# Value projections in four column tiles, and two figures of an instruction planner

## The chip, the core and the metric

The kernel runs on one core of a Trainium2 chip. The time is that of the device, in microseconds (us), from runs of the whole kernel. The core has a matrix engine (PE), a scalar engine for exponentials and gelu (ACT), a vector engine (DVE), GpSimd (POOL) and a queue that issues the DMAs (SP). They run on their own and wait for each other by semaphores.

## The reference, cut to what matters

Two layers, each an attention (A) and a token mixer with an MLP (B), on one sequence of 2048 tokens of 512 features. All 32 heads have 16 features and share one key and one value projection.

```
x = x + A(layernorm(x)); x = x + B(layernorm(x))     # twice, the same weights
A: q = (x @ wq) in 32 heads of 16;  k = x @ wk;  v = x @ wv        # k, v: 2048 x 16
   p = softmax(q k^T / 4);  o = p v;  return o @ wo
B: h = gelu(layernorm(x) @ w1), its four column groups shifted by 1, -1, 2, -2 tokens; x1 = x + h @ w2
   return x1 + gelu(layernorm(x1) @ w3) @ w4
```

## The kernel before

**Attention.** Queries are taken in chunks of 512 tokens (two of 256 at the end of layer 2). A chunk has eight blocks of four heads; a block goes over 16 key tiles of 128. The scores of two heads and one key tile, 128 keys by 1024, are a "half" (two key tiles of 256 queries in the short chunks); there are 2048 halves. Scores are made by row-tiled matmuls (`qk`, L1051), 32 rows each. An exponential is taken in one of two ways. A "unit" (`declare_unit`, L1084) is one ACT instruction over a half (L1100) into one of six EA buffers. A "pair" (`declare_pair`, L1106) takes two DVE instructions that turn scores into the bits of a bf16 power of two (L1121, J, four buffers), and two further versions with added constants (L1131, JK, five buffers), most of them on POOL; the three are weighted by scaled copies of the values (VD). PV (`declare_pv`, L1166) multiplies either by the values, with the values' rows also holding a one, so that the softmax's denominators come out with the sums. Four column tiles of 32 columns accumulate in one PSUM bank per block.

**At a block's end** (`block_end`, L1188) DVE copies the bank (L1214). PE picks the denominators out of the copy (`fz`, L1219 to 1227: four tokens' column tiles for each 128 queries), DVE takes reciprocals (L1231), PE spreads them (L1239), DVE multiplies (L1245), and DMAs move the result to where the output projection reads it.

**Values.** `kv` (L897) makes keys and values of a few token tiles from their normalised, transposed input. Keys are column-tiled (L909). Values (`fv`, L924 to 932) are tokens by features: the tokens are the weights of the array, 128 columns, and WV streams through with 32 columns; four such matmuls sum over the 512 features. DVE copies the 16 used columns (L933) and makes three scaled copies (L938). There are 11 calls: four of four tiles in layer 1's head, seven of one to four tiles between the layers.

**The order of instructions** is written out by a planner in the program itself (`Plan`, L32). Each operation has a duration, a priority and what it reads and writes. The planner simulates the engines, picks at each moment the operation of best priority that it holds ready, and emits for each engine a fixed order with semaphore waits. On the chip the order stands, and only the times differ. What bears on the change:

- A PE operation has a kind: "Q" for row-tiled scores, "P" for column-tiled work, "F" for the whole array. Its planned time is a count of columns at 2.4 per ns; kind P adds 6 ns for each 512 columns. A change of kind costs 0.103 us in the plan (`SWITCH`), and an operation can join those in flight only if its kind is theirs (L224).
- PVs wait until two are ready before a run of kind P is begun for them (`deferred`, L266), or until one has waited for 3 us.
- Where PE would otherwise not be busy enough, the planner puts in matmuls of zeros, fillers (L1062).
- An operation's result counts as ready at its end less `after`, plus a drain (0 for POOL); a reader on PE may start 0.06 us after that (L377, L162 to 172). The engine itself is taken for the whole duration. A POOL instruction at L1131 is planned with 1.12 us.
- Pairs are started when PSUM banks, buffers and DVE's planned queue allow (`assign`, L1312). How many halves become pairs thus comes out of the plan.

Of the kernel before, what the change touches and what calls it, by code (L numbers as in the profile page):

```python
# [31 lines left out]
class Plan:  # L32
# [70 lines left out]
    def op(self, eng, emit, reads=(), writes=(), dur=0.1, prio=None, take=None, give=None,  # L103
           dma=0, out=False, side=True, pe=None, port=False, parts=1, after=0.0):
        o = Op()
        o.eng, o.emit, o.dur, o.take, o.give, o.dma, o.out, o.side = \
            eng, emit, dur, take, give, dma, out, side
        o.pe = pe
        o.port = port
        o.parts = parts  # L110
        o.after = after
        o.feeds = None
        o.seq = len(self.ops)
        o.prio = self.base if prio is None else prio
        o.succ = []
        o.placed = False
        o.start = o.end = None
        o.pos = None
        preds = set()
        for t in reads:  # L120
            r = self.res.get(t)
            if r is not None and r[0] is not None:
                preds.add(r[0])
        for t in writes:
            r = self.res.get(t)
            if r is not None:
                if r[0] is not None:
                    preds.add(r[0])
                preds.update(r[1])
        for t in reads:  # L130
            self.res.setdefault(t, [None, []])[1].append(o)
        for t in writes:
            self.res[t] = [o, []]
        o.preds = preds
        for t in writes:
            if isinstance(t, Late):
                if take is None:
                    t.gates += [p for p in preds if p not in t.ops]
                t.ops.append(o)
        o.ready = self.now  # L140
        o.entry = 0.0
        if self.pace is not None and side:
            if pe is not None:
                self.release += pe[1] * self.pace / 2400.0
                if take is not None:
                    self.entry = self.release
            o.entry = self.entry
        n = 0
        for p in preds:
            if p.placed:  # L150
                o.ready = max(o.ready, self._after(p, o))
            else:
                p.succ.append(o)
                n += 1
        o.npend = n
        self.ops.append(o)
        self.left += 1
        if n == 0:
            self._push(o)
        return o  # L160
# [349 lines left out]
def t_x4(n):  # L510
    return 0.068 + n * 0.26e-3
# [18 lines left out]
class Kernel:  # L530
# [366 lines left out]
    def kv(self, la, tiles, prio=None):  # L897
        op = self.pl.op
        slot = self.slot(la, tiles[0] // 4)
        n0 = (tiles[0] % 4) * 128  # L900
        n = 128 * len(tiles)
        rd = self.yt_tags(la, tiles)
        L = Late()
        for h in range(2):
            def fpe(e, h=h):
                ins = None
                for dc in (2 * h, 2 * h + 1):
                    for g in range(4):
                        ins = e.matmul(self.PB[32 * g:32 * g + 32, L.bank, 0:n], lhsT=self.WK[:, dc, :],  # L909
                                       rhs=self.yt(slot)[:, dc, n0:n0 + n], start=(dc == 0), stop=(dc == 3),  # L910
                                       tile_position=(0, 32 * g), skip_group_check=True)
                return ins
            op("PE", fpe, reads=rd + [("WK",)], writes=[L], pe=("P",) + mm(n, 2)[1:] + (range(4),), prio=prio,
               take=L if h == 0 else None)
        k0 = tiles[0] * 128
        if la == 0 and tiles[0] == 0:
            op("ACT", lambda e: e.copy(self.KT[:, la, k0:k0 + n], self.PB[:, L.bank, 0:n]),
               writes=[L] + [("KT", la, t) for t in tiles], dur=0.0505 + n / 1200, prio=prio, give=L)
        else:
            op("DVE", lambda e: e.tensor_copy(self.KT[:, la, k0:k0 + n], self.PB[:, L.bank, 0:n]),  # L920
               writes=[L] + [("KT", la, t) for t in tiles], dur=t_ps(n), prio=prio, give=L)
        M = Late()

        def fv(e):  # L924
            ins = None
            for i, tb in enumerate(tiles):
                for dc in range(4):
                    ins = e.matmul(self.PB[:, M.bank, 32 * i:32 * i + 32],
                                   lhsT=self.yt(slot)[:, dc, n0 + i * 128:n0 + (i + 1) * 128],
                                   rhs=self.WV[:, dc, :], start=(dc == 0), stop=(dc == 3))  # L930
            return ins
        op("PE", fv, reads=rd + [("WV",)], writes=[M], pe=("F", 240 * len(tiles), 128 * len(tiles)), prio=prio, take=M)
        op("DVE", lambda e: e.tensor_copy(  # L933
            self.VP[:, la, tiles[0]:tiles[0] + len(tiles), 0:16],
            self.PB[:, M.bank, 0:32 * len(tiles)].rearrange("p (t x) -> p t x", x=32)[:, :, 0:16]),
           writes=[M] + [("VP", la, t) for t in tiles], dur=0.14, prio=prio)
        for j in range(3):
            op("DVE", lambda e, j=j: e.tensor_scalar(  # L938
                out=self.VD[:, j, la, tiles[0]:tiles[0] + len(tiles), 0:16],
                in0=self.PB[:, M.bank, 0:32 * len(tiles)].rearrange("p (t x) -> p t x", x=32)[:, :, 0:16],  # L940
                scalar1=self.PARTS[j], scalar2=None, op0=ALU.mult),
               writes=[M] + [("VD", la, t) for t in tiles], dur=0.14, prio=prio, give=M if j == 2 else None)
# [163 lines left out]
    def declare_pair(self, g):  # L1106

        op = self.pl.op  # L1110
        m = self.ndve
        self.ndve += 1
        self.waiting.append(m)
        js = m % self.N_J
        J = self.J[:, js, :]
        for i in range(2):
            h = 2 * g[5] + i
            L = Late()
            op("PE", lambda e, h=h, L=L: self.qk(e, g, h, L.bank), reads=self.inputs(g), writes=[L],
               pe=("Q", 512, 128, (h,)), prio=0.5, side=False, take=L)  # L1120
            o = op("DVE", lambda e, i=i, L=L: e.tensor_scalar(  # L1121
                out=J[:, i * 512:(i + 1) * 512], in0=self.PB[:, L.bank, :],
                scalar1=128 * LOG2E * 0.25, scalar2=float(127 * 128), op0=ALU.mult, op1=ALU.add),
                writes=[L, ("J", js, i)], dur=t_ps(512), prio=1, side=False, give=L)
        jt = [("J", js, 0), ("J", js, 1)]
        es = [(J, jt)]
        for k in (1, 2):
            r = (2 * m + k - 1) % self.N_JK
            self.adds = [p for p in self.adds if not p.placed]
            eng = "POOL" if len(self.adds) < self.ADDS else "DVE"  # L1130
            x = op(eng, lambda e, k=k, r=r: e.tensor_scalar(  # L1131
                out=self.JK[:, r, :], in0=J, scalar1=float(self.STEPS[k]), scalar2=1.0, op0=ALU.add,
                op1=ALU.mult),
               reads=jt, writes=[("JK", r)], dur=t_x4(1024) if eng == "DVE" else 1.12, prio=2, side=False, port=True,
                   after=0.0 if eng == "DVE" else 0.07)
            if eng == "DVE":
                o = x
            else:
                self.adds.append(x)
            es.append((self.JK[:, r, :], [("JK", r)]))  # L1140
        self.pairs.append(o)
        self.add_pv(g, [(self.shaped(ap.bitcast(dt.bfloat16), [2, 512]), tg, k, m) for k, (ap, tg) in enumerate(es)])
# [45 lines left out]
    def block_end(self, la, c, b, end):  # L1188
        op = self.pl.op
        if end == "more":  # L1190
            ap, tags = self.SPILL[b]
            self.last_copy = op("DVE", lambda e: e.tensor_tensor(out=ap, in0=self.PB[:, self.ACC, :], in1=ap,
                                                                 op=ALU.add),
                                writes=[("AC",)] + tags, dur=t_ps(512), prio=0, side=False)
            return
        if end == "spill":
            ap, tags = self.SPILL[b]
            self.last_copy = op("DVE", lambda e: e.tensor_copy(ap, self.PB[:, self.ACC, :]), writes=[("AC",)] + tags,
               dur=t_ps(512), prio=0, side=False)
            return  # L1200
        n = self.size(la, c)
        nq = n // 128
# [3 lines left out]
        am, zm, om = ([(x, i) for i in parts] for x in ("ACCF", "RZ", "OS"))  # L1206
        acc, rz, osm = self.ACCF[:, m * n:m * n + n], self.RZ[:, 4 * nq * m:4 * nq * (m + 1)], self.OS[:, m * n:m * n + n]
        if end == "add":
# [3 lines left out]
               reads=tags, writes=[("AC",)] + am, dur=t_ps(512), prio=0, side=False)  # L1212
        else:
            self.last_copy = op("DVE", lambda e: e.tensor_copy(acc, self.PB[:, self.ACC, 0:n]),  # L1214
               writes=[("AC",)] + am, dur=t_ps(n), prio=0, side=False)
        fin = min(5, self.RUSH[la][c])
        L = Late()

        def fz(e):  # L1219
# [4 lines left out]
                    ins = e.matmul(self.PB[32 * g:32 * g + 32, L.bank, 4 * q:4 * q + 4], lhsT=acc[:, y:y + 32],  # L1224
                                   rhs=self.SELC, start=True, stop=True, tile_position=(0, 32 * g))
            return ins
        op("PE", fz, reads=am + [("SELC",)], writes=[L], pe=("P", 100 * nq, 4 * nq, range(4)), prio=fin, take=L)

        def frec(e):
            with self.nc.allow_low_precision("the reciprocals feed a bf16 matmul"):  # L1230
# [349 lines left out]
```

## Time and profile before

| | |
|---|---|
| time, median of 9 runs | 1534.26 us (1533.68 to 1534.59) |
| the profiled execution: its own time, its span | 1534.59 us, 1532.8 us |
| busy: PE, ACT, DVE, POOL | 98%, 96%, 84%, 76% |
| exponentials on ACT (L1100) | 1471 |
| DVE conversions (L1121), two for a pair | 1154 |
| JK on POOL, on DVE (L1131) | 982, 172 |
| value matmuls (L928), whole array | 128 |
| denominator matmuls (L1224), in 72 sums | 1024 |
| fillers on PE (ones by zeros) | 952 matmuls, 86.9 us busy |

Busy times are of one profiled execution. A matmul's record includes its way through the array, so records overlap, and PE's share is not a share of its peak; what one matmul takes from the next is read from the distance of their starts. A line such as `x1471 | 1353.7, 1152 | 16.1` gives the number of instructions, their busy time in us, the mean of one in ns, and the engine's idle time before them in us, followed by what ended it. The chain that ended last goes back from the last instruction to what released it, step by step. PEld is the weight load of PE, which overlaps with its matmuls.

### The profile page before, as it was taken

The page shows a single profiled execution, that of the slowest core. Times are in us where ns is not written, and L with a number is a line of the kernel's source. Part 1 is how long each engine was busy: PE and PEld are TensorE (multiplying, and loading weights), DVE is VectorE, ACT ScalarE, POOL GpSimd, SP SyncE. Part 2 cuts the span into 40 slices and gives each one's busy share as a digit, 9 for nine tenths or more (in the row PEclk, how much of TensorE's full clock was granted, in tenths as well). Part 3 has the DMA queues.
Part 4 walks back from the last instruction along what each step waited for, and adds up shares of the span by engine and source line. Part 5 has one row for each costly group of instructions (what it writes and reads, how often), then busy time and mean ns, then how long its engine had stood idle before and what let it go on. Part 6 is the DMA issues. An engine that isn't in the chain of part 4 may idle for free.

```text
span 1532.8 us, 66274 instructions
## 1 busy us (share of the span) xinstructions
PE 1495.2 (98%) x30137; PEld 648.8 (42%) x30137; DVE 1282.1 (84%) x2265; ACT 1469.8 (96%) x1563; POOL 1171.7 (76%) x1243
## 2 busy tenths in 40 slices
PE   8999999999999999999999999999999999999999
PEld 4333333443433444333434434334443334454565
DVE  8888888889988889988886788988788896898863
ACT  7999999999999989999999999999999999999972
POOL 2789999878888858987675489888788886788651
DMA  6100100001000001000000000010000000000000
GB/s 208 30 5 5 20 6 6 4 6 19 6 4 6 6 4 20 6 5 2 3 2 3 3 8 11 6 20 4 13 14 7 5 6 11 19 10 7 6 14 23
DMA packets 32153, 21.70 MB, mean 14 GB/s; under 512 B 12672, under 2 KB 31360, under 8 KB 31872
## 3 DMA queue, kind: packets, MB, share of 16 engines
q1 hardware_dynamic: 31872, 17.47, 4.8%
q8 instruction: 235, 3.85, 1.1%
q14 instruction: 46, 0.38, 0.1%
HBM read 7.90 MB, written 2.10 MB: 7 GB/s over the span
## 4 chain that ended last, share of the span: by engine, by line
ACT 75%; PE 15%; POOL 6%; DVE 3%; issue 1%; DMA 0%; SPq 0%; POOLq 0%
ACT EA L1100 70%; PE PB L653 6%; POOL JK L1131 4%; PE PB L1056 4%; PE PB L1180 3%; ACT G L1513 2%; ACT L1100 1%; DVE J L1121 1%; ACT GP L1433 1%; POOL SM L788 1%; ACT L1433 1%; POOL ZR L1404 1%; ACT L1513 1%; DMA X<-in_A_x_dram 0%; DVE G L1508 0%
## 5 line engine op out<-in xcount | busy, mean ns | idle before, releaser
L1100 ACT ACTIVATE EA<-PB 128x1024 bf16<-128x1024 f32 x1471 | 1353.7, 1152 | 16.1 <-PE PB L1180 10.3
L1131 POOL TENSOR_SCALAR JK<-J 128x1024 uint16<-128x1024 uint16 x982 | 1036.6, 1056 | 253.1 <-DVE J L1121 160.5
L1121 DVE TENSOR_SCALAR J<-PB 128x512 uint16<-128x512 f32 x1154 | 745.2, 681 | 120.3 <-PE PB L1056 117.5
L1056 PE MATMUL PB<-QT,KT 32*128 32x512 bf16 (+1 forms) x4608 | 614.3, 360 | 19.8 <-ACT EA L1100 8.3
L1180 PE MATMUL PB<-EA,VP 128*32 128x256 bf16 (+1 forms) x6636 | 381.9, 263 | 1.9 <-DVE ACCF L1214 1.2
L1056 PEld LDWEIGHTS PB<-QT,KT 32*128 32x128 bf16 x4608 | 163.4, 91 | 400.8 <-ACT EA L1100 335.1
L1180 PE MATMUL PB<-JK,VD 128*32 128x256 bf16 (+1 forms) x5160 | 301.3, 266 | 5.2 <-POOL JK L1131 3.6
L1180 PEld LDWEIGHTS PB<-EA,VP 128*32 128x32 bf16 x6636 | 157.5, 95 | 136.4 <-issue 105.7
L1180 PEld LDWEIGHTS PB<-JK,VD 128*32 128x32 bf16 x5160 | 119.2, 94 | 145.2 <-issue 81.6
L653 PE MATMUL PB<-ZT,W 128*32 128x512 bf16 (+2 forms) x2816 | 173.2, 342 | 0.8 <-DVE ZT L861 0.3
L1180 PE MATMUL PB<-J,VD 128*32 128x256 bf16 (+1 forms) x2580 | 164.8, 264 | 0.6 <-issue 0.3
L1131 DVE TENSOR_SCALAR JK<-J 128x1024 uint16<-128x1024 uint16 x172 | 121.2, 712 | 3.0 <-PE PB L1180 0.4
L653 PE MATMUL PB<-W,G 128*32 128x512 bf16 x1624 | 102.4, 380 | 0.1
L653 PE MATMUL PB<-ONES,NIL 128*32 128x512 bf16 x952 | 86.9, 391 | 3.2 <-DVE ST L768 0.9
L1508 DVE CAST G<-PB 128x512 bf16<-128x512 f32 (+2 forms) x126 | 71.8, 580 | 20.2 <-PE PB L653 19.4
L1180 PEld LDWEIGHTS PB<-J,VD 128*32 128x32 bf16 x2580 | 64.2, 95 | 43.2 <-issue 34.5
L653 PEld LDWEIGHTS PB<-ZT,W 128*32 128x32 bf16 x2816 | 61.6, 96 | 37.3 <-issue 23.5
L788 POOL TENSOR_TENSOR SM<-SM,MH 128x2 f32<-128x2 f32 (+1 forms) x69 | 48.0, 698 | 22.8 <-DVE SM L790 16.0
L1513 ACT ACTIVATE G<-G 128x1792 bf16<-128x1792 bf16 x29 | 47.0, 1686 | 12.6 <-DVE G L1508 12.5
L653 PEld LDWEIGHTS PB<-W,G 128*32 128x32 bf16 x1624 | 42.3, 96 | 36.3 <-issue 10.9
L1245 DVE TENSOR_TENSOR OS<-ACCF,PB 128x512 bf16<-128x512 bf16 (+1 forms) x72 | 44.6, 619 | 7.1 <-PE PB L1239 6.9
L768 DVE BATCH_NORM_STATS2 ST<-X 128x6 f32<-128x512 f32 (+1 forms) x64 | 43.3, 681 | 3.1 <-DMA X<-in_A_x_dram 2.5
(108 smaller groups left out, 865.0 us busy)
## 6 DMA issues: line engine op xcount, KB each, us to landing
OT<-OS SPq DMA_DIRECT2D x424, 8.0 KB, 1.8
W<-in_B_w_dram SPq DMA_DIRECT2D x2, 1792.0 KB, 14.1
X<-in_A_x_dram SPq DMA_DIRECT2D x8, 256.0 KB, 6.7
QT<-QS SPq DMA_DIRECT2D x32, 64.0 KB, 2.5
out_dram<-OUTB SPq DMA_DIRECT2D x16, 128.0 KB, 1.7
OT<-OS SPq DMA_DIRECT2D x104, 4.0 KB, 2.2
W<-in_B_w_dram SPq DMA_DIRECT2D x2, 512.0 KB, 8.6
WQ<-in_A_wq_dram SPq DMA_DIRECT2D x1, 512.0 KB, 6.2
```

The source lines that it names most:

```text
L653: ins = e.matmul(self.PB[32 * g:32 * g + 32, bank, 0:n], lhsT=lhsT[:, 32 * g:32 * g + 32], rhs=rhs, start=start, stop=stop, tile_position= ...
L768: op("DVE", lambda e, tb=tb: e.bn_stats(self.ST6[:, tb, :], src(tb)), reads=[tagf(tb)], writes=[("ST", tb)], dur=0.606, prio=prio)
L788: op("POOL", lambda e: e.tensor_tensor(out=out, in0=src, in1=self.MH[:, 0, a:b], op=ALU.pow), reads=tags + [("MH",)], writes=tg(r), dur=0. ...
L1056: ins = e.matmul(self.PB[:, bank, j * n:(j + 1) * n], lhsT=self.KT[32 * h:32 * h + 32, la, (kb + j) * 128:(kb + j + 1) * 128], rhs=self.QT ...
L1100: o = q.feeds = op("ACT", lambda e: e.activation(self.EA[:, ea, :, :], self.PB[:, b0:b0 + 2, :], ACTF.Exp, scale=0.25), writes=bk + [("EA" ...
L1121: o = op("DVE", lambda e, i=i, L=L: e.tensor_scalar(out=J[:, i * 512:(i + 1) * 512], in0=self.PB[:, L.bank, :], scalar1=128 * LOG2E * 0.25 ...
L1131: x = op(eng, lambda e, k=k, r=r: e.tensor_scalar(out=self.JK[:, r, :], in0=J, scalar1=float(self.STEPS[k]), scalar2=1.0, op0=ALU.add, op1 ...
L1180: ins = e.matmul(self.PB[32 * x:32 * x + 32, self.ACC, p * hw:p * hw + hw], lhsT=v[:, la, kb + j, :], rhs=ap[:, i, j * w + u * hw:j * w + ...
L1245: op("DVE", lambda e: e.tensor_tensor(out=osm, in0=acc, in1=self.PB[:, M.bank, 0:n], op=ALU.mult), reads=am, writes=[M] + om, dur=t_ps(n), ...
L1433: op("ACT", lambda e: e.activation(self.GP[:, par, :, 2:2 + n], self.GP[:, par, :, 2:2 + n], ACTF.Gelu_apprx_tanh), reads=gt, writes=gt, d ...
L1508: op("DVE", lambda e, f=f, L=L: e.tensor_copy(self.G2[:, f, 0:n], self.PB[:, L.bank, 0:n]), writes=[L] + [(x, f, i) for x in ("G2", "GE") ...
L1513: op("ACT", lambda e, i=i: e.activation(self.G2[:, :, i * 128:(i + 1) * 128], self.G2[:, :, i * 128:(i + 1) * 128], ACTF.Gelu_apprx_tanh), ...
```

## The change

Three edits. Values: each whole-array matmul becomes four column-tiled ones, with 32 tokens as the weights of each column tile; they write the same places of the bank, and the planner has them as kind P with 256 columns for each token tile, where it had kind F with 240. Denominator sums: their planned columns go from 100 to 60 for each 128 queries; the instructions are the same. JK on POOL: `after` is dropped, so a result counts as ready at 1.12 us from its start, where it was 1.05. The last two change what the planner believes, and all three the order that it writes.

```
                 for dc in range(4):
-                    ins = e.matmul(self.PB[:, M.bank, 32 * i:32 * i + 32],
-                                   lhsT=self.yt(slot)[:, dc, n0 + i * 128:n0 + (i + 1) * 128],
-                                   rhs=self.WV[:, dc, :], start=(dc == 0), stop=(dc == 3))
+                    for g in range(4):
+                        y = n0 + i * 128 + 32 * g
+                        ins = e.matmul(self.PB[32 * g:32 * g + 32, M.bank, 32 * i:32 * i + 32],
+                                       lhsT=self.yt(slot)[:, dc, y:y + 32], rhs=self.WV[:, dc, :], start=(dc == 0),
+                                       stop=(dc == 3), tile_position=(0, 32 * g), skip_group_check=True)
             return ins
-        op("PE", fv, reads=rd + [("WV",)], writes=[M], pe=("F", 240 * len(tiles), 128 * len(tiles)), prio=prio, take=M)
+        op("PE", fv, reads=rd + [("WV",)], writes=[M], pe=("P", 256 * len(tiles), 128 * len(tiles), range(4)), prio=prio, take=M)
...
-               reads=jt, writes=[("JK", r)], dur=t_x4(1024) if eng == "DVE" else 1.12, prio=2, side=False, port=True,
-                   after=0.0 if eng == "DVE" else 0.07)
+               reads=jt, writes=[("JK", r)], dur=t_x4(1024) if eng == "DVE" else 1.12, prio=2, side=False, port=True)
...
-        op("PE", fz, reads=am + [("SELC",)], writes=[L], pe=("P", 100 * nq, 4 * nq, range(4)), prio=fin, take=L)
+        op("PE", fz, reads=am + [("SELC",)], writes=[L], pe=("P", 60 * nq, 4 * nq, range(4)), prio=fin, take=L)
```

## The prediction

> **What bounds the kernel now.** I read the page's busy shares first, then the chain that ended last, then the groups of instructions, then the waits, and last the timeline around the lines that the diff touches.
>
> ```profile
> span 1532.8 us, 66274 instructions
> PE 1495.2 (98%) x30137; PEld 648.8 (42%) x30137; DVE 1282.1 (84%) x2265; ACT 1469.8 (96%) x1563; POOL 1171.7 (76%) x1243
> ACT 75%; PE 15%; POOL 6%; DVE 3%; issue 1%; DMA 0%; SPq 0%; POOLq 0%
> ```
>
> The first two lines are the page's totals, the third its chain by engine. PE shows 98%, but it holds 952 matmuls of ones times zeros, fillers that the planner puts in where PE has nothing due: 238 groups of four, about 0.215 us apart, some 51 us. So ScalarE is the bound: three quarters of the chain is on it. The other 25% are stretches in which the chain runs through PE, POOL and DVE and ScalarE is served just in time; only there is a nanosecond of PE or POOL worth a nanosecond.
>
> ```profile
> L1100 ACT ACTIVATE EA<-PB 128x1024 bf16<-128x1024 f32 x1471 | 1353.7, 1152 | 16.1 <-PE PB L1180 10.3
> L1131 POOL TENSOR_SCALAR JK<-J 128x1024 uint16<-128x1024 uint16 x982 | 1036.6, 1056 | 253.1 <-DVE J L1121 160.5
> L1121 DVE TENSOR_SCALAR J<-PB 128x512 uint16<-128x512 f32 x1154 | 745.2, 681 | 120.3 <-PE PB L1056 117.5
> 36.15 172.43 ACT EA L1100 x188
> ```
>
> Three groups of the page and one piece of the chain. There are 2048 halves of score tiles; 1471 go through ScalarE's exponential, and 1154/2 = 577 as "pairs" through DVE and POOL. The chain's piece gives the exponential's pitch, 172.43/188 = 0.917 us. A pair more or less is therefore 0.917 us of ScalarE.
>
> ```profile
> POOL JK L1131 <- PE PB L1180: 20.4, 19, 2.7
> PEld PB L1180 <- POOL JK L1131: 45.2, 166, 0.8
> ACT EA L1100 <- PE PB L1180: 10.3, 4, 6.0
> ```
>
> From the waits (total us, times, longest). POOL waits 19 times for a PV matmul to free one of the five JK buffers; PE's weight loads wait 166 times for POOL; ScalarE stands still 10.3 us behind PV, 5.97 us of it at 554.75 and 3.62 us at 852.65, both at the end of an attention block.
>
> ```profile
> 20.00 0.60 PE L909 MATMUL PB<-YT,WK 128*32 128x512 bf16 x8
> 20.54 0.57 PE L928 MATMUL PB<-WV,YT 128*128 128x32 bf16 x16
> 21.03 0.29 PE L852 MATMUL PB<-IDENT,ZR 128*32 128x128 bf16 x6
> 553.22 0.28 PE L1180 MATMUL PB<-JK,VD 128*32 128x256 bf16 x4
> 553.43 0.27 PE L928 MATMUL PB<-WV,YT 128*128 128x32 bf16 x4
> 553.63 0.38 PE L1056 MATMUL PB<-QT,KT 32*128 32x512 bf16 x1
> 555.18 0.25 PE L1224 MATMUL PB<-SELC,ACCF 128*32 128x4 bf16 x16
> 555.29 0.38 PE L1180 MATMUL PB<-EA,VP 128*32 128x256 bf16 x5
> ```
>
> Three timeline stretches (start, duration with the pipeline's tail, engine, line): two value projections with their neighbours, and one denominator sum.
>
> [...] 16 value matmuls of 32 columns start over 390 ns, 26 ns each, and groups of four concurrent denominator matmuls of 4 columns start 25 ns apart. [...] the trace has 105 to 106 ns extra between a column-tiled group and a row-tiled QK (215 against 110, 321 against 215). [...] Here a load takes 96 ns with 128 columns and 96 with 32, so I give that no price. [...] The trace has POOL's semaphore at 1.053 us after the start of a 1.044 us JK record, and the waiting PV matmul starting at 1.098 us, while the next POOL instruction comes at 1.122 us.
>
> **Part 1, value projections.** 128 matmuls in 11 calls become 512, in 128 groups of four. A group of four starts every 25 ns with 4 columns and every 56 ns with 128 (identity matmuls, L1239). I take 26 ns for 32 columns, as now, so the stream of one four-tile call stays 16 x 26 = 416 ns. The bounds are 25 ns, and 56 ns, which would cost 128 x 30 ns = 3.9 us of PE. What goes is the switch to the untiled array: about 98 ns going in (312 ns after a 512-column group, against 213 to 216) and 80 ns coming out (105 against 25). By the neighbours on PE in the trace: three calls between column-tiled work save 177 ns each; six with QK behind them save 98 and pay about 22 more for QK's own switch, net 75; one with QK ahead saves 81; one between two QKs about 52. Sum: 531 + 450 + 81 + 52 = 1.11 us of PE. On the path at the 25% share: -0.3 us. The 768 added PE instructions issue no DMA of their own; the four evacuations behind each call on DVE are unchanged. That DVE waited only 1.4 us for these matmuls.
>
> **Part 2, denominator sums.** No instruction changes. The planner charged 400/2400 = 167 ns plus 6, and will charge 106 with those 6; the trace has 103 from first start to the next group's start where both are column-tiled. For two-tile sums it is 53, against 83 plus 6. 56 sums times 67 ns and 16 times 33 ns free 4.3 us of planned PE time. The hardware already runs that way, so the only gain is better order: 4.3 x 0.25 = -1.1 us; bounds -4.3, and +1 for an order that leans on PE more than it can bear.
>
> **Part 3, POOL results.** The planner now has a JK result at start + 1.12 - 0.07, and lets PE read it 0.06 later: 1.11, the trace's 1.098. Afterwards it says 1.18, some 80 ns later than the truth, for each of 982 results. Two things follow.
>
> First, a gain. By the matmul starts, 370 groups of JK PV start later than the usual spacing after the group ahead, by 19.4 us in all; taking at most 80 ns of each leaves 9.7 us that a more cautious plan need not lose. x 0.25 = -2.4 us; bounds 0 and -4.9.
>
> Second, a loss. PE serves PV between bursts of QK, which come once per exponential. A result that is believed 70 ns later misses its visit with a chance of 0.070/0.917 = 7.6%, so 982 x 7.6% = 75 results are put off by one visit. Each keeps its JK buffer (five in all, two and a half pairs) and its J buffer (four) for 0.9 us more. Queued behind it are POOL's next JK and, on POOL's same queue, the layer norms' small powers; the next pair's DVE conversion waits for J. Where ScalarE is well ahead (75%) I count nothing, because POOL has 253 us of idle time. In the other 25%, 19 results each cost half a pair, 0.46 us: +8.6 us. The bounds are 0 (only 19 of 982 POOL starts wait for PV now, 20.4 us) and 75 x 0.46 = 34 us, which would need POOL full throughout. At a block's end the last JK also holds back the accumulator's copy, and the next block's PV behind it; the six EA buffers cover about 5.5 us of that.
>
> **The sum**, against the profiled execution's own 1534.6 us (span 1532.8 and 1.8 around it): -0.3 - 1.1 - 2.4 + 8.6 = +4.8, 1539.4 us. That execution is 0.3 above the median, so I write 1539.
>
> **The rivals.** A (0.40) is this sum, 1536 to 1544: five or so fewer pairs.
> B (0.36), faster: the slack of part 3 gives back more than it costs. Place: JK PV groups on PE. If other work is put ahead of each late group, the whole 19.4 us is used, x 0.25 = 4.9; with parts 1 and 2 -6.3, 1528. It decides when fewer than 8 of the slips cost half a pair (8 x 0.46 = 3.7 against 3.8 of gains). For it: POOL is idle 24%, and only 2% of its starts wait for a buffer. Against it: ScalarE has at most 11.8 us of gaps between 36 and 1475 us, so the floor is near.
> C (0.14), no change: 1534. Exponentials cover all of it, PE's time turns into fillers, and the number of pairs stays within three of 577. For it: 238 fillers. Against it: an order written out from times is made anew from the first value projection, at 13.7 us, on; it is unlikely to keep its count.
> D (0.10), slower by more: one more block end like that at 554.75, where POOL's six JK in a row ended at 551.36 and PE was in a run of 72 MLP matmuls until 553.2. One such is 6 us on top of A: 1545, two 1551.
> That the change doesn't do what it says is part of C: the value matmuls might not overlap by fours, 3.9 us of PE, x 0.25 = 1 us.
>
> **How the numbers follow.** What can't be told from no change is 0.2%, 3 us. Faster is B, 0.36; same C, 0.14; slower A and D, 0.50. The likeliest is A, 1539, own range 1536 to 1544. The 8-in-10 range reaches over most of B (6 us below its figure would need both of the long stalls gone) and over D with one or two stalls: 1525 to 1552.
>
> **What the changed profile would show.** Part 1: 512 matmuls 128*32 by 32 at that line, 26 ns from group to group, about 25 ns from the last to a column-tiled neighbour, no 100 ns ahead of the first. Part 2: sums still 103 ns. Part 3: fewer than 100 weight loads waiting for POOL, and less than 30 us there. A: about 1476 exponentials and 572 pairs, POOL waiting more than 20.4 us for PV. B: 1468 or fewer exponentials. D: a gap of over 4 us before an exponential at a block's end that is not there now. I am wrong if the count of exponentials stays and the time moves: then stalls at block ends, or the tail of 57.7 us after the last exponential, have decided, which I took as unchanged.

## The result, and the profile after

The changed kernel takes 1543.34 us (median of 9 runs, 1541.69 to 1544.87) against 1534.20 us for the kernel before on the same chip (29 runs): a ratio of 1.0062, 95% interval 1.0053 to 1.0070. It is 9.1 us slower. The forecast was slower, 1539 us, within 1525 to 1552.

The page of the kernel after: totals, the granted clock in 40 slices, the chain by engine, and the three groups that were read before.

```profile
span 1541.6 us, 67024 instructions
PE 1502.9 (97%) x30517; PEld 648.3 (42%) x30517; DVE 1282.6 (83%) x2257; ACT 1476.1 (96%) x1570; POOL 1151.4 (75%) x1223
PEclk9999999999999999999999999999999999999999
...
ACT 70%; PE 21%; DVE 6%; POOL 2%; issue 1%; DMA 0%; POOLq 0%
...
L1102 ACT ACTIVATE EA<-PB 128x1024 bf16<-128x1024 f32 x1478 | 1360.0, 1147 | 20.3 <-PE PB L1058 14.1
L1133 POOL TENSOR_SCALAR JK<-J 128x1024 uint16<-128x1024 uint16 x962 | 1016.0, 1056 | 285.1 <-DVE J L1123 196.7
L1123 DVE TENSOR_SCALAR J<-PB 128x512 uint16<-128x512 f32 x1140 | 736.3, 682 | 118.6 <-PE PB L1058 114.9
```

Seven more halves go to ScalarE: 1478 exponentials and 570 pairs. And there is a clock line, which the page of before doesn't have: somewhere PE did not get its full clock (a mean of 0.998 in the profiled execution). The waits say that POOL was not held up by PV, as the prediction had it.

```profile
PEld PB L1181 <- issue: 230.1, 986, 2.4
POOL JK L1133 <- DVE J L1123: 196.7, 147, 9.8
PEld PB L1181 <- POOL JK L1133: 37.8, 142, 0.6
POOL JK L1133 <- PE PB L1181: 10.8, 13, 2.4
```

POOL's waits for PV fell from 20.4 to 10.8 us. But "issue", time in which the engine waits for nothing that the profile shows, now has one of 2.4 us. Two pieces of PE's timeline in the first 30 us show where:

```profile
12.60 0.51 PE L930 MATMUL PB<-WV,YT 128*32 128x32 bf16 x42
14.79 0.32 PE L930 MATMUL PB<-WV,YT 128*32 128x32 bf16 x22 [1.68 <-issue]
...
25.22 0.28 PE L1181 MATMUL PB<-EA,VP 128*32 128x256 bf16 x2
27.73 0.29 PE L1181 MATMUL PB<-EA,VP 128*32 128x256 bf16 x2 [2.22 <-issue]
```

PE stops in the middle of a value projection, after 42 of 64 matmuls with the same inputs, and in the middle of a PV, after two of four. No semaphore can end a wait there, since neither operation waits inside. Busy times by stage (the last columns are granted clock, share of the DMA engines and GB/s), first before, then after:

```profile
5.00:15.00 10.00, 8.43 (x184) 3.76 (x180) 8.51 (x28) 3.27 (x3) 2.20 (x3) 1.00 1.05 338
15.00:20.00 5.00, 4.66 (x120) 2.44 (x120) 5.00 (x19) 4.91 (x6) 1.38 (x2) 1.00 1.05 394
20.00:25.00 5.00, 5.00 (x135) 2.56 (x130) 5.00 (x19) 3.51 (x5) 1.02 (x2) 1.00 1.08 354
```

```profile
5.00:15.00 10.00, 7.74 (x224) 3.90 (x220) 7.97 (x25) 3.27 (x3) 2.21 (x3) 1.00 1.07 348
15.00:20.00 5.00, 4.66 (x102) 1.83 (x88) 4.31 (x16) 3.71 (x4) 1.38 (x2) 0.64 1.04 395
20.00:25.00 5.00, 5.00 (x160) 2.65 (x152) 2.96 (x9) 2.11 (x3) 0.00 (x0) 0.68 1.07 348
```

After the first stop the granted clock is 0.50 for 6.8 us (16.4 to 23.2 us; 0.64 and 0.68 are means over their stages). All this happens while the DMA engines are full of inputs and weights: their busy share reads 1.04 to 1.08 in these stages of both kernels, and 0.11 to 0.16 from 25 to 30 us. At 50 us, 35 exponentials had begun before, and 28 after. So two things have to be told apart: what the head loses, and what the new order of the rest costs.

The matmuls up to each stop, counted in the traces, gave the lead. In the kernel after, PE stops after its 223rd and its 479th matmul. The kernel before has one stop of this kind, 0.58 us at 27.74 us, also after its 479th. Other kernels below add one after the 351st. The distances are 128 matmuls: with as many weight loads, 256 instructions. On the page of before, queue 8, "instruction", moved 3.85 MB in 235 packets of 16 KB; PE's 2 x 30137 instructions make 256.5 for each packet. On the page of after it has 238 packets, for 2 x 30517: 256.4. The same step shows in the stops and in the packets, so this queue is read here as the fetch of PE's instructions, a block of 256 for a packet. The times agree: in the kernel after, packets of this queue start at 12.28 and 25.12 us, take 1.14 and 1.10 us, and PE goes on 2.51 and 2.61 us after their starts, at 14.79 and 27.73; in the kernel before, one starts at 25.18, and PE goes on 2.56 us after that. Later it doesn't show in PE's time: in the kernel before, the packets that start from 40 to 85 us are 5.7 to 7.7 us ahead of the first matmuls of their blocks, counted on by 128, and no wait of its matmuls for "issue" after 30 us is over 0.28 us.

### The profile page after: what moved, and what is told of

It is laid out like the page before. It is cut to its first block, busy times and chain, and to the rows that moved or that the text cites. A ratio compares the mean times of both kernels' runs of the same rounds, so it can differ in the third digit from the quotient of the medians.

```text
span 1541.6 us, 67024 instructions
## 1 busy us (share of the span) xinstructions
PE 1502.9 (97%) x30517; PEld 648.3 (42%) x30517; DVE 1282.6 (83%) x2257; ACT 1476.1 (96%) x1570; POOL 1151.4 (75%) x1223
## 4 chain that ended last, share of the span: by engine, by line
ACT 70%; PE 21%; DVE 6%; POOL 2%; issue 1%; DMA 0%; POOLq 0%
ACT EA L1102 65%; PE PB L653 7%; PE PB L1058 7%; PE PB L1181 6%; ACT G L1514 3%; DVE J L1123 2%; ACT L1102 1%; POOL JK L1133 1%; ACT GP L1434 1%; DVE ST L768 1%; ACT L1514 1%; DVE JK L1133 1%; PE PB L852 1%; ACT L1434 0%; DVE X L1391 0%
## 5 line engine op out<-in xcount | busy, mean ns | idle before, releaser
L1133 POOL TENSOR_SCALAR JK<-J 128x1024 uint16<-128x1024 uint16 x962 | 1016.0, 1056 | 285.1 <-DVE J L1123 196.7
L1123 DVE TENSOR_SCALAR J<-PB 128x512 uint16<-128x512 f32 x1140 | 736.3, 682 | 118.6 <-PE PB L1058 114.9
L1058 PE MATMUL PB<-QT,KT 32*128 32x512 bf16 (+1 forms) x4608 | 621.2, 360 | 18.9 <-ACT EA L1102 7.4
L1133 DVE TENSOR_SCALAR JK<-J 128x1024 uint16<-128x1024 uint16 x178 | 132.4, 753 | 3.8 <-PE PB L1181 1.9
L653 PE MATMUL PB<-ONES,NIL 128*32 128x512 bf16 x1004 | 92.4, 395 | 1.8 <-DVE Y L805 0.4
L653 PEld LDWEIGHTS PB<-ZT,W 128*32 128x32 bf16 x2816 | 62.1, 96 | 35.1 <-issue 23.5
L653 PEld LDWEIGHTS PB<-W,G 128*32 128x32 bf16 x1624 | 37.8, 96 | 40.8 <-issue 11.1
```

The source lines that it names most:

```text
L653: ins = e.matmul(self.PB[32 * g:32 * g + 32, bank, 0:n], lhsT=lhsT[:, 32 * g:32 * g + 32], rhs=rhs, start=start, stop=stop, tile_position= ...
L1058: ins = e.matmul(self.PB[:, bank, j * n:(j + 1) * n], lhsT=self.KT[32 * h:32 * h + 32, la, (kb + j) * 128:(kb + j + 1) * 128], rhs=self.QT ...
L1123: o = op("DVE", lambda e, i=i, L=L: e.tensor_scalar(out=J[:, i * 512:(i + 1) * 512], in0=self.PB[:, L.bank, :], scalar1=128 * LOG2E * 0.25 ...
L1133: x = op(eng, lambda e, k=k, r=r: e.tensor_scalar(out=self.JK[:, r, :], in0=J, scalar1=float(self.STEPS[k]), scalar2=1.0, op0=ALU.add, op1 ...
```

## The experiments

Theory F: PE runs out of instructions in the head, because the tiled value projections bring it to the block's end sooner, while the fetch has to share full DMA engines (busy share 1.04 to 1.08 up to 25 us). Theory P: the new order is what costs. Of the orders, the number of exponentials was known before each run, and the expectations use it.

### Old order, new tiles

```
# the kernel before, with the changed loop over g in fv; the planner's line stays
  pe=("F", 240 * len(tiles), 128 * len(tiles))
```

> The order of the kernel before, instruction for instruction, with the value matmuls alone written as four column tiles (the planner still believes the old ones); 1471 exponentials and 577 pairs as before. Theory F (PE runs out of instructions in the head because the tiled value projections are 128 instructions where 32 stood[...]): about 1540 us, a stop of over 1 us in PE within the first 30 us that no semaphore explains, mean clock below 1.000, and some 6 us of ScalarE gaps more before 50 us. Theory P (only the new order costs): 1533 to 1535 us, clock 1.000.

Measured: 1540.87 us (1538.76 to 1541.72), ratio 1.0038 (1.0025 to 1.0051), clock 0.998. PE's timeline:

```profile
12.41 0.51 PE L930 MATMUL PB<-WV,YT 128*32 128x32 bf16 x42
14.53 0.32 PE L930 MATMUL PB<-WV,YT 128*32 128x32 bf16 x22 [1.61 <-issue]
```

Theory F holds: every engine has its old order and the same 1471 exponentials, and tiling alone costs 6.3 us here, with stops of 1.61 and 1.90 us after the same two matmuls, the 223rd and the 479th. Most of that is not the clock: one of the five executions had a mean clock of 1.000, to three places, and still took 1539.24 us. Of the gaps expected on ScalarE before 50 us only 3.7 us showed in the profiled execution (14.4 against 10.7), which was the fastest of the five; 30 exponentials had begun at 50 us, five fewer than before, and those are worth 4.6 us.

### New order, old tiles: in the head, and everywhere

```
# the changed kernel; in the second, the whole-array matmuls in all calls
  for dc in range(4):
      if la: (four tiles, as changed)
      else:  (one whole-array matmul, as before)
```

> The order of the changed kernel, instruction for instruction (1478 exponentials, 570 pairs), with the four value projections of layer 1's head written as whole-array matmuls again, those between the layers tiled. Theory F: 1543.3 less some 6 us, so about 1537 us, clock 1.000, no long stop of PE in the head. Theory P: 1543 us.

> The order of the changed kernel with all value projections written as whole-array matmuls: what the order alone costs. Theory F: within 0.5 us of the run with only the head undone, about 1537 us; the seven calls between the layers save at most 0.6 us by tiling. Theory P: 1543 us.

Measured: 1537.58 us (ratio 1.0019, 1.0012 to 1.0027) and 1537.84 us (1.0022, 1.0013 to 1.0031) against 1534.57, clock 1.000 in both. So both theories hold in part: the change's 9.1 us are 6.3 for the tiles in the head and 3.0 to 3.3 for the order; the sum is 9.3 to 9.6. With the seven calls between the layers tiled the time is 0.26 us lower, which the runs can't tell from nothing. These kernels still stop, without losing the clock; with the old head, after the 351st and the 479th matmul:

```profile
20.72 0.57 PE L852 MATMUL PB<-IDENT,ZR 128*32 128x128 bf16 x26 [0.62 <-issue]
27.46 0.61 PE L653 MATMUL PB<-YT,WQ 128*32 128x512 bf16 x6 [0.96 <-issue]
```

The traces also show why more instructions cost so much here. The fetch's packets start at 12.55, 18.84 and 25.18 us in the kernel before, and at 12.28, 18.51 and 25.12 in the changed one: the blocks come at nearly the same times in both. The 224th matmul starts at 14.53 us with the old head and at 14.79 with the tiled one; but the first had waited 0.18 us for it and the second 1.68, and the second was only two thirds through a projection that the first had finished.

What the order costs, from the traces of before and of the kernel with the old head: seven more exponentials, 6.4 us; ScalarE's idle time before 50 us 12.0 against 10.7, +1.3; its gaps ahead of exponentials after that 8.8 against 12.2, -3.4; the tail after the last exponential 57.0 against 57.7, -0.7. That is 3.6; the spans differ by 3.2.

### Each part alone

```
# part 1: values as changed, planned as changed; the other two as before
# part 3: side=False, port=True   (no after=)
# part 2: pe=("P", 60 * nq, 4 * nq, range(4))
```

> Part 1 alone, planned and written as in the changed kernel (1469 exponentials by its order, 579 pairs). Theory F: two exponentials less are worth 1.8 us, the head costs about 6: 1538 us, clock below 1.000. Theory P, by the count of exponentials: 1532 us. The prediction's part 1: -0.3 us, 1534.

> Part 3 alone. Theory S (the prediction's: late-believed JK results slip a visit and cost pairs and waits): 1538 us or more, POOL waiting more than 20.4 us for PV. Theory O (what counts is which order comes out, not the size or sign of the edit): its order has 1470 exponentials and 578 pairs, one exponential less than before, so 1533.6 us, apart from ScalarE's gaps, which O can't tell ahead: up to 5 us either way. Both: fewer than 30 us of weight loads waiting for POOL.

> Part 2 alone, the planned length of the denominator sums as the trace has it. The prediction: -1.1 us, 1533.4. Theory O: its order has 1475 exponentials, four more than before, 1538 us, with the gaps open by up to 5 us either way. If part 2 is what costs in the changed order (7 more exponentials), this count is where most of it comes from.

Measured: part 1 alone 1550.61 us (1.0106, 1.0091 to 1.0121, against 1534.57), part 3 alone 1541.28 (1.0045, 1.0030 to 1.0060) and part 2 alone 1538.26 (1.0026, 1.0016 to 1.0036), both against 1534.35. Alone they cost 16.0, 6.9 and 3.9 us, 26.8 together; in one kernel 9.1. Costs of this kind don't add.

Part 1 alone has two exponentials less and is 16 us slower, 12.6 us more than theory F had for it. ScalarE's timeline shows what neither theory had named:

```profile
805.63 1.28 ACT L1515 ACT_TABLE_LOAD   x1
813.81 4.88 ACT L1515 ACTIVATE G<-G 128x1792 bf16<-128x1792 bf16 x3 [6.90 <-DVE G L1510]
...
826.23 1.28 ACT L1515 ACT_TABLE_LOAD   x1
837.43 3.29 ACT L1515 ACTIVATE G<-G 128x1792 bf16<-128x1792 bf16 x2 [9.92 <-DVE G L1510]
```

Two batches of gelus stand in ScalarE's order ahead of exponentials, and wait 6.90 and 9.92 us for their input from DVE; nothing else runs on ScalarE in these waits. Fetch stops of 1.61, 1.42 and 3.25 us in the head add to it.

Part 3 alone is the test of the prediction's largest term. Its waits:

```profile
POOL JK L1131 <- DVE J L1121: 180.5, 135, 6.6
...
PEld PB L1179 <- POOL JK L1131: 35.1, 135, 0.7
POOL JK L1131 <- PE PB L1179: 19.3, 13, 8.1
```

It has one pair more, not fewer; POOL waits for PV less often (13 times for 19) and no longer in all (19.3 for 20.4 us). The weight loads' wait for POOL came down to 35.1, not under 30. So theory S got the time, 1538 us or more, but not by its mechanism, which falls: neither lost pairs nor more waiting for PV is there. Theory O got the count and missed the time: 1541.3 lies outside its 1533.6 within 5. The 7.0 us of span are made of gaps ahead of exponentials after 50 us (13.8 us against 12.2; the two largest, 4.43 us at 351.8 and 4.40 at 780.4, are together no longer than the 5.97 and 3.62 of before), one gelu that waits 3.82 us at 837.3, and a tail of 59.9 for 57.7 us: 1.6 + 3.8 + 2.2, less 0.9 for the exponential saved, gives 6.7.

Part 2 alone has four more exponentials, 3.7 us, and 13.8 us of gaps for 12.2; here O's 1538 us came.

### Edits that mean nothing

```
- after=0.0 if eng == "DVE" else 0.07
+ after=0.0 if eng == "DVE" else 0.08       # and, in the second kernel, 0.069
```

> The kernel before, with POOL's results believed ready 0.08 us ahead of the pitch's end where it had 0.07: a tenth of part 3's change, and to the other side. Theory S: a hundredth of a microsecond of belief moves nothing, 1534.5 us within 1. Theory O: the order is made anew and has 1467 exponentials, 1531 us, gaps open by up to 5 us either way.

> The kernel before, with 0.069 where it had 0.07: one nanosecond of planner's belief, nothing that the hardware can know of. Theory S: 1534.5 us within 1. Theory O: 1477 exponentials by its order, six more than before, 1540 us, gaps open by up to 5 us either way.

Measured: 1549.93 us (1.0102, 1.0087 to 1.0117) and 1550.91 us (1.0112, 1.0095 to 1.0128). One nanosecond in the planner's belief costs 16.6 us. The four values of `after` give, in order, 1549.9 (0.08), 1534.3 (0.07), 1550.9 (0.069) and 1541.3 us (0): no slope, as good as a draw each time. Theory S's "within 1" fell in both. Theory O had the counts right, but both times lie outside the 5 us that it allowed for gaps: 1531 and 1540 were forecast, and with 0.08 the kernel has four exponentials fewer and is 15.6 us slower. Of the four orders that O forecast, it got one time. That a new order comes out is shown; that its count of exponentials tells the time is not.

With 0.069 the exponentials are six more, 5.5 us, and a batch of gelus that before stood behind the last exponential now stands ahead of the last eleven:

```profile
1471.48 1.28 ACT L1513 ACT_TABLE_LOAD   x1
1472.78 6.46 ACT L1513 ACTIVATE G<-G 128x1792 bf16<-128x1792 bf16 x4
1479.25 1.28 ACT L1100 ACT_TABLE_LOAD   x1
1480.55 10.51 ACT L1100 ACTIVATE EA<-PB 128x1024 bf16<-128x1024 f32 x11
```

That puts 9.0 us (6.46 and two table loads) in front of them, and the tail, 58.1 us, gets nothing back. With 0.08 the same batch stands ahead of the last twelve, and one gelu waits long for DVE besides; here the tail is 4.0 us shorter:

```profile
751.85 1.91 ACT L1433 ACTIVATE GP<-GP 128x2048 bf16<-128x2048 bf16 x1 [10.45 <-DVE GP L1429]
1472.87 6.46 ACT L1513 ACTIVATE G<-G 128x1792 bf16<-128x1792 bf16 x4
```

In both kernels half the clock is then granted for a while among the last exponentials, for 6.8 us from 1482.7 (0.08, mean clock 0.998) and for 3.4 us from 1475.1 (0.069, mean clock 0.999), with no fetch stop near.

### The weights put off

```
-  load(self.WO, ...); load(self.W1, ...); ... load(self.W4, ...)
+  the same five, each with reads=[("QT", 0, 7)]: behind the first moves of queries
```

> The run with the old order and tiled value matmuls, with the loads of WO, W1, W2, W3 and W4 (5.2 MB, first needed after 200 us) put on SP's queue behind the first moves of queries, so some 45 us later; every other engine's order is the same, instruction for instruction. Theory F1 (the instruction fetch is late because it shares the DMA engines with these loads): the stops of 1.6 and 1.9 us fall under 0.7 us, the clock is 1.000, and the time is 1533 to 1535 us. Theory F2 (the fetch is late by itself, whatever the DMA engines do): the stops stay, 1541 us. Against both: the loads now meet the fetches from 45 to 65 us[...].

> The changed kernel with the same five loads put off. Theory F1: its order alone remains, as in the run with the new order and the old tiles, 1537.6 us, clock 1.000. Theory F2: 1543 us.

> The kernel before with the same five loads put off. Theory F1: its one stop in the head, 0.58 us at 27.7 us, goes, worth at most 0.6 us: 1534 us, at best 1533.5. Theory F2: 1534.4 us. If the loads harm the fetches between 45 and 65 us, up to 2 us more.

Measured, against 1534.02 us: old order with new tiles 1532.48 us (0.9990, 0.9981 to 0.9999), the changed kernel 1535.72 us (1.0012, 1.0005 to 1.0018), the kernel before 1532.02 us (0.9987, 0.9980 to 0.9993). PE's timeline and the stages of the first of them:

```profile
12.60 0.51 PE L930 MATMUL PB<-WV,YT 128*32 128x32 bf16 x42
13.40 0.32 PE L930 MATMUL PB<-WV,YT 128*32 128x32 bf16 x22 [0.29 <-issue]
```

```profile
5.00:15.00 10.00, 9.13 (x264) 4.60 (x260) 9.17 (x33) 3.96 (x4) 2.30 (x4) 1.00 0.63 207
15.00:20.00 5.00, 4.66 (x133) 2.30 (x130) 5.00 (x16) 4.99 (x6) 1.28 (x2) 1.00 0.02 5
20.00:25.00 5.00, 5.00 (x162) 2.70 (x158) 5.00 (x17) 3.80 (x5) 1.38 (x2) 1.00 0.01 3
```

The same instructions in the same order, with idle DMA engines from 15 us on (busy share 0.02 and 0.01): the stop after the 223rd matmul is 0.29 us, the one after the 479th is gone, the clock stays at 1.00, and 8.4 us come back, 2.0 of which the kernel before gains as well. The packet of the fetch starts at 10.86 us where it started at 12.03, and PE goes on at 13.40 where it went on at 14.53: 2.54 and 2.50 us after that start. So F1 holds: in the crowd the packet starts 1.17 us later, and what follows takes no longer. In the changed kernel the two stops are 0.15 us and none.

With the crowd gone, new tiles cost 1532.48 - 1532.02 = 0.46 us on the old order; the two kernels' ranges overlap (1532.00 to 1533.21, 1531.74 to 1532.63), so this is at most a small loss, and no gain. The whole change then costs 1535.72 - 1532.02 = 3.7 us, nearly all of it the order. The kernel before with its weights put off beats both kernels of this case, by 2.0 and 11.3 us. It gained more than its one stop of 0.58 us, which was all that was expected: ScalarE's idle time before 50 us fell from 10.7 to 8.3 us. The input rows had shared the DMA engines with the weights too: they landed a median of 6.7 us after their issue before, 5.3 us here. How the 2 us divide between the two was not tried. In these times no harm from the loads between 45 and 65 us shows.

## Why the prediction was right, and where it was wrong

**Direction and size.** Slower was held the likeliest, and 1543.3 lies in the likeliest case's own range, 1536 to 1544. The count of pairs went the way of case A: seven fewer, where five or so were written. But the sum came out near by other terms than its own: the 8.6 us that made it "slower" did not come in the way it was argued, and the 6.3 us of the head were in no term. That 1543.3 fell where it did was luck.

**What bounds the kernel** stood: seven more halves on ScalarE, at 0.917 us each, are 6.4 us, the largest term of the order's account, of which shorter gaps gave 3.4 back; the tail moved by 0.7 us only. The page's idle time puts the gaps from 36 to 1476 us at 12.8, where the prediction read 11.8. The share of 25%, by which every gain was cut, was not tested.

**Part 1.** The step that failed is "The 768 added PE instructions issue no DMA of their own". They do, as the traces read here: they come by DMA themselves, 256 at a time (three packets more, 238 for 235, with the old order and new tiles), and 4 x 96 of the 768 fall in the head, half of them before 25 us, where the DMA engines are full (busy share 1.04 to 1.08). That term was nothing in the sum and measured 6.3 us. The smaller figure was off as well: 26 ns for a group of four was taken. The trace has 25 to 29 ns for the first seven groups of a call and mostly 32 to 38 after that, one 59: 64 matmuls start over 511 ns, where the 16 before took 390. The switches went about as forecast (behind a 512-column group 205 to 212 ns where 311 to 312 stood; ahead of column-tiled work 25 to 34, one 142, where 105 and 106 stood); by that they leave an estimated 0.2 of their 1.11 us. Free of the fetch the part shows no gain: 0.46 us slower, with overlapping ranges, where 0.3 us faster was forecast.

**Part 2.** "Only better order" was forecast at -1.1 us, bounds -4.3 and +1. Alone it cost 3.9 us. The planner's figure did become right; the order that came of it had four more exponentials. That a truer figure gives a better order was an assumption, and no line of the profile stood behind it.

**Part 3.** The loss of 8.6 us, results that slip a visit and hold buffers, is the term that made the forecast "slower", and its mechanism fell: alone, the edit kept all its pairs, and POOL waited for PV less often. Alone it cost 6.9 us all the same, by one gelu out of place, a longer tail and slightly longer gaps. The gain of 2.4 us from fewer late starts was not seen in the time; weight loads waiting for POOL fell from 166 to 142 and from 45.2 to 37.8 us (35.1 alone), not below 100 and 30.

**The rivals.** B fell with its gain. C's argument against itself was the right one: an order written from times is made anew from the first value projection on, and doesn't keep its count. D, a stall like the one at 554.75, did not come: the largest gap ahead of an exponential after 50 us, up to the tail, is 3.07 us. What the prediction lacked was to carry C's sentence through to the sum. After a new order, the change of time is as good as a draw; five such orders here (1537.7 with the tiles undone, 1538.3, 1541.3, 1549.9 and 1550.9) were all slower than before, and no sum over the edit's nanoseconds tells one from the other. If better and worse were equally likely, five worse of five would come once in 32 times; so the order of before is probably a good one of its kind. How it came to be so is not on record.

## What to carry to other kernels

Where a planner writes the order, measure an edit twice: with the old order kept and the new instructions put in, and with the new order and the old instructions; the two costs here were 6.3 and 3.0 us, and only the first belongs to the instructions. A change of a nanosecond in a planner's figure is the yardstick for how much any new order may move. And count instructions as traffic: a wait called "issue" in the middle of one operation, at a fixed number of instructions from the last such wait, was here an engine out of instructions, and bulk loads that weren't needed yet were better kept out of its way: putting them off was worth 8.4 us with the tiled projections on the old order, 2.0 without.

## What the hardware showed that was not expected

- Queue 8, "instruction", moved one packet of 16 KB for about 256 of PE's instructions, 128 matmuls with their loads (60274 in 235 packets before, 61034 in 238 after; a packet took 0.88 to 1.55 us). Where PE stopped in the head, it was after matmuls 223, 351 or 479, in whichever kernel, for up to 3.25 us. The stops shrank or went when other DMA traffic did (1.61 to 0.29 us, 1.90 to none, with a DMA busy share of 0.63 for 1.08 from 5 to 15 us, and 0.01 to 0.02 for 1.04 to 1.07 from 15 to 25).
- In the changed kernel and in the one with old order and new tiles, a stop of 1.6 to 1.7 us ending near 14.6 us was followed by 6.8 us at half clock (in the changed one 0.50 was granted from 16.4 to 23.2 us). With the values alone the same stop was not, but one of 3.25 us was followed by 3.4 us at half clock. Stops of 1.42, 1.90 and 2.22 us were not followed by one, nor was any of up to 1.0 us in the head. With `after` at 0.08, 6.8 us at half clock began 0.9 us after PE had waited 3.32 us for an exponential; with 0.069, 3.4 us began where PE's waits of the last 3 us had been 0.41, 0.58 and 0.20 us. So the length of one stop doesn't decide it; what does was not tried.
- A group of four column tiles, 128 rows by 32 columns each, starts 25 to 29 ns after the last one in the first seven groups of a call and mostly 32 to 38 ns after that. Over 64 matmuls that is 511 ns, not faster than 16 whole-array matmuls of the same work at 26 ns each, 390 ns.
